# A gated mix of an S5 state-space layer and Hedgehog linear attention: K's weight in halves of rows, four x tiles ahead of V's weight, K products ahead of V's, and a new order list with the later loads in it

## The chip, the core and the metric

The kernel runs on one core of a Trainium2 chip. The metric is the device time of one execution in microseconds (us). The engines are named as the profile names them: PE is TensorE's matmuls and PEld its weight loads, DVE is VectorE, ACT is ScalarE, POOL is GpSimd, SP is SyncE, which here issues DMAs only.

## The reference

Shapes: S = 2048 rows of x, D = 512 columns, state size 512, 32 heads of 16. All inputs and the output are bf16.

```python
x = A_x                                              # [1, 2048, 512]
g = sigmoid((x * gate_w).sum(-1, keepdims=True))
# a: S5. Lam_bar = exp(dt * Lam), B_bar = ((Lam_bar - 1) / Lam)[:, None] * B, all complex
h[t] = Lam_bar * h[t - 1] + x[t] @ B_bar.T
a = 2 * (hseq @ C.T).real + x * Dskip
# b: Hedgehog attention without a mask
q, k, v = split(x @ wqkv)                            # 32 heads of 16
pq, pk = q @ w_phi, k @ w_phi                        # per head
phi_q = [softmax(pq), softmax(-pq)]; phi_k = [softmax(pk), softmax(-pk)]
kv = phi_k.T @ v; z = phi_k.sum(s)
b = ((phi_q @ kv) / (phi_q @ z + 1e-6)) @ wo
out = g * a + (1 - g) * b
```

## The kernel before

**Layout.** x is loaded transposed: 16 DMA transposes of 128 rows each, issued by SyncE, fill xT, [128 partitions, 4 blocks of D, 2048 columns]. The rows are taken by residue: tile ti holds rows 4c + r with r = ti // 4, so that the state-space recurrence is done four steps at a time (the step matrices of Lam_bar's powers are 128x128 diagonals in `dg`, and a scan on DVE carries every fourth step).

**Folded weights.** w_phi is folded into the weights of K and Q before any product: pk = x @ (Wk BD), where BD is block-diagonal with w_phi's 16x16 blocks. For K this is done at the head of the run: `st_B` builds BD out of w_phi (Wc) and a block mask, the steps W0 to W3 (`st_W`) transpose K's natural weight on TensorE into WTk, and f0 to f3 (`st_f`, `fold`) multiply WTk by BD and evict a quarter of Wk2 each. Q's weight is loaded transposed by DMA (WTq) and folded later by w0 to w3.

**Steps and the order list.** Nearly all work is written as generators, one for each step, and the string ORDER says which step is advanced next. A token is a step's name; "@3" gives the PSUM bank it takes, ":D" evicts with DVE instead of ACT, ":A" issues an output store from ACT's queue. Each engine runs its instructions in the order in which the list emits them, without any reordering, except GpSimd, whose order the framework chooses. The steps that matter here:

- V and V2 transpose the small vectors (vec_n: Lambda and log_dt; vec_m: Dskip and gate_w) that GpSimd loads; U, P, P2 to P4 and M compute the state-space parameters from them on DVE, ACT and GpSimd, i0 to i3 the tables of sines and cosines, D the diagonals.
- k0 to k15, v0 to v15, q0 to q15: the products of x tile n with the K, V and Q weights (four matmuls of 512 columns), evicted to Xq, vxb and Xq.
- x, n, e, s with a number: maximum tree, minimum tree, exponentials, sums and normalization of the two softmaxes for a pair of K tiles; A, B and X, N, E, S the same for Q. a0 to a7 accumulate kv, z and the gate's logits in two PSUM banks.
- p (for example p30): LBT = the B matrices (Bn_r, Bn_i) times the diagonals; g: the inputs of the recurrence (xT with BrT, BiT and LBT); z: the scan; h, c, K, r, b: later state-space matrices; y, o, t: the output, 16 tiles.
- F:n issues n spin matmuls of 128 columns on a bank of their own.

**Loads.** All loads are issued ahead of the list. ACT's queue issues K's weight (one DMA of 512 KB into the tile whose name is C2r), w_phi (Wc) and V's weight (Wv). SyncE's queue issues x tiles 0 to 7, the natural B matrices Bn_r and Bn_i (512 KB each), the transposed BrT and BiT (four DMAs each), x tiles 8 to 15, WTq (four; the trace names it H), CrT and CiT (four each) and Wo. SyncE's queue later carries the transposes of the query features (phT), of the attention outputs (oT) and most output stores. GpSimd's queue loads the five small vectors.

Of the kernel before, what the change touches and what calls it, by code (L numbers as in the profile page):

```python
# [26 lines left out]
k3 x0 i1 M v2 V2 v7@1 n0 i2 k2 k7 v3@4 i1 i3 x0 n0 x0 i3 k4 k5 v4@7 i2 n0 i2 k6@2 i2 x1 n0 i3 x1 v0@0 i3 D v4 v3 p22@3  # L27
x1 n1 v5@5 p00@6 x1 n1 x1 i3 x2 L n1 x2 p30@7 v7:D e0 p20@4 x2 D v5 n1 n1 p10@1 p20 n2 p02@5 p30 p10 x2 e0 D n2 s0 v0
v6@4 k6 g101@7 p00 x2 s0 x3 n2 s0 g001@1 g000@0 n2 s0 e1 e1 g001 n2 s1 s0 s0 e2 g100@2 p22 g101 g001 x3 n3 gw s0 e2 n3
k9@6 x3 v6 g100 a0@31 k9 g000 a0 s1 n3 s1 n3 k8@4 g000 x3 s1 s1 s1 g100 k10@6 s2 k8 x3 n3 p12@0 e3 g101 k11@2 s1 e3 x4  # L30
k11 a1 s2 g010@4 n4 k10 a1 s2 g011@7 n4 x4 s2 n4 x4 n4 s3 g010 g011 s2 x4 s3 x4 n4 x5 k12@2 s3 p02 s2 e4 n5 k13@6 x5
e4 s3 x5 s2 n5 s3 g010 g011 s4 a2 k12 g011 x5 n5 s3 p32@5 k13 s4 n5 a2 s3 x5 n5 x6 g010 z0 s4 w0@2 n6 w0 p32 v9@7 w3@6
z0 g111@4 p12 g210@2 n6 w3 s4 e5 e5 w1@5 s5 w1 a3 v8@0 x6 k14@6 s4 z0 g111 g110@5 a3 n6 z0 v9 s5 v8 k15@7 k14 s4 v11@0
z0 x6 x6 z0 k15 s4 n6 w2@6 g110 w2 g201@7 x6 g111 g111 x7 g110 z0 a4 x7 c01@6 z0 g200@4 g110 z1 s5 q1@5 v11 z1 g311@0
s5 x7 s5 n6 s5 c01 n7 g201 e6 z1 g211@6 a4 z1 g201 x7 g200 v10@7 z1 z1 e6 g200 z0 g210 q0@4 g211 g210 s5 q1 n7 v12@5
q0 q3@4 x7 n7 s6 z0 g210 n7 s6 n7 g211 s6 v10 nA xA g301@2 s6 a5 e7 z1 g300@7 g211 q3 e7 nA v14@6 z1 xA z2 nA q2@4 v14
a5 z2 g300 xA s6 s7 q2 z2 s6 s7 z2 g301 g300 xA s7 g311 g301 v12 g310@6 xA g311 z1 nA c11@4 z1 nA eA z2 nB s7 z2 c03@7
c12@2 g310 xB g311 eA q15@5 c12 s6 c03 s7 g310 h01@0 nB q15 g310 sA c10@2 z2 s7 h01 c11 c13@7 xB nB v13@5 z3 xB h11@6
z2 c10 z3 a6 z2 sA z2 h11 q9@0 c02@4 v13 sA q9 xB a6 nB c13 h10@2 q6@5 c02 v15@0 z3 q12@7 q10@6 q8@4 xB v15 sA nB
# [29 lines left out]
def kernel(  # L69
# [45 lines left out]
    def evac(out_ap, in_ap):  # L115
        if sel["eng"] == "act":
            nc.scalar.copy(out=out_ap, in_=in_ap)  # L117
        else:
            nc.vector.tensor_copy(out=out_ap, in_=in_ap)
# [109 lines left out]
    nc.sync.dma_start(out=Bn_r[:], in_=A_B_re.rearrange("(j p) d -> p j d", p=P))  # L229
    nc.sync.dma_start(out=Bn_i[:], in_=A_B_im.rearrange("(j p) d -> p j d", p=P))  # L230
    for kt in range(KT):
        nc.sync.dma_start_transpose(out=BrT[:, kt, :], in_=A_B_re[:, kt * P:(kt + 1) * P])
        nc.sync.dma_start_transpose(out=BiT[:, kt, :], in_=A_B_im[:, kt * P:(kt + 1) * P])
    for ti in range(8, NTI):
        x_load(ti)
    for j in range(KT):
        nc.sync.dma_start_transpose(out=WTq[:, j, :], in_=B_wqkv[:, j * P:(j + 1) * P])
    for kt in range(KT):
        nc.sync.dma_start_transpose(out=CrT[:, kt, :], in_=A_C_re[:, kt * P:(kt + 1) * P])
        nc.sync.dma_start_transpose(out=CiT[:, kt, :], in_=A_C_im[:, kt * P:(kt + 1) * P])  # L240
    nc.sync.dma_start(out=Wo[:], in_=B_wo.rearrange("(k p) n -> p k n", p=P))
# [20 lines left out]
    mask16 = stg.tile([P, 8], F32, name="mask16", bufs=1)  # L262
    nc.vector.tensor_reduce(out=mask16[:], in_=identf[:].rearrange("p (g e) -> p g e", e=16), axis=AX.X, op=ALU.add)
# [12 lines left out]

    def st_W(j):
        pt = bank([P, KT, P], BF16, "ptw")
        for dtile in range(KT):
            nc.tensor.transpose(pt[:, dtile, :], wk_nat[:, dtile, j * P:(j + 1) * P], ident[:])  # L280
        yield
        evac(WTk[:, j, :], pt[:].rearrange("p a b -> p (a b)"))
        yield

    def st_V():
# [460 lines left out]
    def st_t(n):  # L746
# [8 lines left out]
        else:  # L755
# [5 lines left out]
    small1, big1 = (lambda: sk), (lambda: fk)  # L761
    small3, big3 = (lambda: pools["sq"][1]), (lambda: pools["eq"][1])
    st = {"V": st_V(), "V2": st_V2(), "U": st_U(), "P": st_P(), "P2": st_P2(), "P3": st_P3(), "P4": st_P4(), "B": st_B(), "gw": st_gw(),
          "M": st_M(), "D": st_D(), "L": st_L(), "G": st_G(), "Y": st_Y(), "END": st_END()}
    for j in range(4):
        st.update({f"W{j}": st_W(j), f"f{j}": st_f(j), f"w{j}": st_w(j), f"i{j}": st_i(j), f"z{j}": st_z(j), f"r{j}": st_r(j),
                   f"b{j}": st_b(j), f"K{j}": st_K(j), f"p{j}0": st_p(j, 0), f"p{j}2": st_p(j, 2)})
        for e in range(2):
            st.update({f"c{e}{j}": st_c(e, j), f"h{j}{e}": st_h(j, e), f"g{j}0{e}": st_g(j, 0, e), f"g{j}1{e}": st_g(j, 1, e)})
# [57 lines left out]
```

## Time and profile before

| | |
|---|---|
| time, median of 3 runs | 167.55 us (167.46 to 167.75) |
| the profiled execution: span, first to last instruction | 166.1 us |
| median minus span | 1.45 us |
| busy share PE / PEld / DVE / ACT / POOL | 95% / 50% / 87% / 69% / 6% |
| mean granted TensorE clock | 0.994 |
| HBM read / written | 2.64 MB / 2.10 MB |
| K's weight: issue, landing | 0.80 us, 5.15 us |
| V's weight: issue, landing | 1.81 us, 7.70 us |
| x tiles 0, 1, 2, 3: landing | 6.25, 8.58, 10.82, 11.19 us |
| first product of x (v1) on TensorE | 9.67 us |

The span is read from the trace; the device time of a run is a little longer than the span of its instructions. Busy times of matmuls overlap, since they are pipelined: a matmul of 512 columns shows 379 ns, but the next starts 216 ns after it. Engine names with a q (SPq, ACTq) are the queues' instructions, which issue or wait. "xT <- in_A_x_dram" reads: out, in.

### The profile page before, as it was taken

The page shows a single profiled execution, that of the slowest core. Times are in us where ns is not written, and L with a number is a line of the kernel's source. Part 1 is how long each engine was busy: PE and PEld are TensorE (multiplying, and loading weights), DVE is VectorE, ACT ScalarE, POOL GpSimd, SP SyncE. Part 2 cuts the span into 40 slices and gives each one's busy share as a digit, 9 for nine tenths or more (in the row PEclk, how much of TensorE's full clock was granted, in tenths as well). Part 3 has the DMA queues.
Part 4 walks back from the last instruction along what each step waited for, and adds up shares of the span by engine and source line. Part 5 has one row for each costly group of instructions (what it writes and reads, how often), then busy time and mean ns, then how long its engine had stood idle before and what let it go on. Part 6 is the DMA issues. An engine that isn't in the chain of part 4 may idle for free.

```text
span 166.1 us, 3051 instructions
## 1 busy us (share of the span) xinstructions
PE 157.6 (95%) x1088; PEld 82.3 (50%) x1109; DVE 143.7 (87%) x354; ACT 114.8 (69%) x236; POOL 9.6 (6%) x28
## 2 busy tenths in 40 slices
PE   7689999999999999999999999999999999999990
PEld 7444455455465454454454554545446445445440
DVE  4379999999999999999999999999999996818410
ACT  3389999999898268578965966876888356423331
POOL 8218200000000000000000000000000000000000
PEclk9999999999999999999999999999999999999997
DMA  4969945464444200000000019212296585478542
GB/s 111 267 121 281 142 99 97 95 98 95 95 105 85 98 0 6 0 0 0 0 4 0 0 24 181 52 32 63 65 132 154 162 189 129 119 174 216 128 125 95
DMA packets 50830, 15.94 MB, mean 96 GB/s; under 512 B 46208, under 2 KB 50816, under 8 KB 50816
## 3 DMA queue, kind: packets, MB, share of 16 engines
q1 hardware_dynamic: 48064, 13.77, 39.8%
q10 hardware_dynamic: 2592, 1.98, 4.4%
q8 instruction: 8, 0.13, 0.3%
q14 instruction: 6, 0.05, 0.1%
q0 software_dynamic: 160, 0.01, 0.1%
HBM read 2.64 MB, written 2.10 MB: 29 GB/s over the span
## 4 chain that ended last, share of the span: by engine, by line
PE 84%; DVE 8%; DMA 3%; POOL 2%; issue 1%; ACT 1%; POOLq 0%
PE pgq L552 8%; PE py L750 8%; PE pgq L555 8%; PE py L705 8%; PE pq L429 8%; PE py L706 8%; PE pv L429 5%; PE py L712 4%; PE pk L429 4%; DMA vec_n<-in_A_log_dt_dram 3%; PE kvacc L527 3%; PE pn L728 3%; PE pk L674 2%; PE pk L675 2%; DVE psi L406 2%; DVE mxk L464 1%
## 5 line engine op out<-in xcount | busy, mean ns | idle before, releaser
L429 PEld LDWEIGHTS <-xT 128*128 128x128 bf16 x192 | 18.1, 97 | 20.8 <-DMA xT<-in_A_x_dram 0.7
L136 ACT ACTIVATE EEk<-EEk 128x1024 bf16<-128x1024 bf16 x20 | 21.0, 1070 | 0.8 <-DVE EEk L480 0.8
L737 DVE SCALAR_TENSOR_TENSOR on<-pn,RG,rd 128x256 bf16<-128x256 f32 x32 | 14.4, 474 | 3.2 <-ACT rd L136 1.7
L429 PE MATMUL pv<-Wv,xT 128*128 128x512 bf16 x62 | 16.0, 379 | 0.3 <-DMA xT<-in_A_x_dram 0.2
L750 PE MATMUL py<-Wo,oT 128*128 128x512 bf16 x62 | 15.8, 379 | 0.1
L555 PE MATMUL pgq<-xT,LBT 128*128 128x512 bf16 x60 | 15.5, 379 | 0.2
L429 PE MATMUL pq<-Wq,xT 128*128 128x512 bf16 x61 | 15.6, 379 | 0.1
L429 PE MATMUL pk<-Wk,xT 128*128 128x512 bf16 x61 | 15.1, 379 | 0.2
L136 ACT ACTIVATE EEq<-EEq 128x1024 bf16<-128x1024 bf16 x12 | 11.8, 1044 | 3.3 <-DVE EEq L480 3.3
L136 ACT ACTIVATE ld<-pn 128x16 f32<-128x16 f32 x32 | 4.7, 182 | 12.6 <-PE pn L728 12.6
L706 PE MATMUL py<-Wv,H 128*128 128x512 bf16 x31 | 11.7, 379 | 0.1
L705 PE MATMUL py<-Wk,H 128*128 128x512 bf16 x31 | 11.7, 379 | 0.1
L705 PE MATMUL py<-C2r,H 128*128 128x512 bf16 x31 | 11.7, 379 | 0.0
L117 ACT CAST Xq<-pq 128x512 bf16<-128x512 f32 x16 | 9.2, 589 | 3.6 <-PE pq L429 3.4
L117 ACT CAST uv<-pgq 128x512 bf16<-128x512 f32 x16 | 9.3, 588 | 3.4 <-PE pgq L560 2.3
L706 PE MATMUL py<-C2i,H 128*128 128x512 bf16 x30 | 11.4, 379 | 0.1
L756 DVE TENSOR_SCALAR ot<-py,G 128x512 bf16<-128x512 f32 x5 | 3.7, 747 | 8.4 <-PE py L750 8.4
L117 ACT CAST vx<-pv 128x512 bf16<-128x512 f32 x15 | 8.7, 598 | 2.6 <-PE pv L429 2.6
L754 ACT ACTIVATE ot<-py,G 128x512 bf16<-128x512 f32 x11 | 7.4, 678 | 4.5 <-PE py L750 4.5
L117 ACT CAST Xq<-pk 128x512 bf16<-128x512 f32 x16 | 9.2, 601 | 1.4 <-PE pk L429 1.4
L464 DVE TENSOR_TENSOR smk<-smk 128x512 bf16<-128x512 bf16 (+2 forms) x30 | 9.8, 327 | 0.0
L500 DVE TENSOR_TENSOR EEk<-EEk,rck 128x2048 bf16<-128x2048 bf16 x8 | 9.7, 1214 | 0.0
(179 smaller groups left out, 348.6 us busy)
## 6 DMA issues: line engine op xcount, KB each, us to landing
out_dram<-ot SPq DMA_DIRECT2D x9, 128.0 KB, 2.1
out_dram<-ot ACTq DMA_DIRECT2D x7, 128.0 KB, 2.1
C2r<-in_B_wqkv_dram ACTq DMA_DIRECT2D x1, 512.0 KB, 4.4
Wv<-in_B_wqkv_dram ACTq DMA_DIRECT2D x1, 512.0 KB, 5.9
Bn_r<-in_A_B_re_dram SPq DMA_DIRECT2D x1, 512.0 KB, 5.1
Bn_i<-in_A_B_im_dram SPq DMA_DIRECT2D x1, 512.0 KB, 6.0
Wo<-in_B_wo_dram SPq DMA_DIRECT2D x1, 512.0 KB, 3.8
xT<-in_A_x_dram SPq DMA_TRANSPOSE x16, 3.9
```

Source lines behind the costliest of these rows:

```text
L117: nc.scalar.copy(out=out_ap, in_=in_ap)
L136: ins = nc.scalar.activation(**kw)
L429: MM(out=pt[:], lhsT=xT[:, kt, ti * P:(ti + 1) * P], rhs=W[:, kt, :], start=(kt == 0), stop=(kt == KT - 1))
L464: VT(out=t[:], in0=cur[:, :, :, 0:n, :], in1=cur[:, :, :, n:2 * n, :], op=op)
L500: VT(out=E5, in0=E5, in1=rc[:].to_broadcast([P, L, 2 * NB, Dh, 4]), op=ALU.mult)
L552: MM(out=pgq[:], lhsT=BT[:, kt, js], rhs=xT[:, kt, r1 * NC:(r1 + 1) * NC], start=(kt == 0), stop=False)
L555: MM(out=pgq[:], lhsT=LBT_[:, kt, js], rhs=xT[:, kt, (r1 - 1) * NC:r1 * NC], start=False, stop=(r1 == 1 and kt == KT - 1))
L705: MM(out=py[:], lhsT=src[:, j, 0, off:off + P], rhs=cr[:, j, :], start=(j == 0), stop=False)
L706: MM(out=py[:], lhsT=src[:, j, 1, off:off + P], rhs=ci[:, j, :], start=False, stop=False)
L737: nc.vector.scalar_tensor_tensor(out=on[:, 2 * hf:2 * hf + 2].rearrange("p g h e -> p (g h) e"), in0=pns[hf][:, :, 0:Dh], scalar=RG[:, ti: ...
L750: MM(out=py[:], lhsT=oT[:, g, :], rhs=Wo[:, g, :], start=False, stop=(g == HG - 1))
L754: nc.scalar.mul(out=ot[:], in_=py[:], mul=G[:, ti:ti + 1])
```

## The change

- K's weight is loaded in two DMAs of 256 rows each, alone on ACT's queue. Step W(j) now transposes the four blocks of rows 128 j to 128 j + 127 and writes them as a column block of WTk, so W0 and W1 read the first half only, and fold f(d) reads what W(d) wrote alone.
- w_phi goes to SyncE's queue as its first load; x tiles 0 to 3 follow, then V's weight, then x tiles 4 to 7.
- The loads behind these (x tiles 8 to 15, Bn, BrT, BiT, WTq, CrT, CiT, Wo) become steps of the list: l8 to l15, NR and NI, R and I, Q, C, O. They are issued in the list's order: NI l11 NR I3 l10 l15 l9 l8 I1 I0 I2 l13 l12 l14 R3 R1 R0 R2 Q2 Q1 Q0 C5 Q3 C2 C3 C4 C7 C6 C1 C0, and O between the last two phT transposes of the first query tiles.
- The identities are made first on GpSimd, the block mask is bf16, and BD is built by one DVE instruction.
- ORDER is new throughout. At its head, all four folds stand ahead of the transpose V, and TensorE's products begin k0 k1 k2 k3 v1 v0 k5 k4 v7 k7, where they began v1 v2 k1 k0 k5 k3 k2 k7 k4 v7. It has six spins between W0 and W1 and six ahead of v2, in place of eight and one ahead of and behind f3. One V eviction and three output scalings move from DVE to ACT, one fold's eviction from ACT to DVE.

```diff
-B B F:36 W2@0 W2 W1@1 W1:D W0@2 W0:D W3@3 B W3 B F:8 f3@4 F:1 V@5 V f3 f0@6 f2@7 P f0 U P f2 P2 f1@0 U f1 v1@1 P2 v2@2
-k1@3 k0@5 P2 P2 U V2@4 k5@6 k3@7 P P2 P4 P4 U P4 i0 k2@0 P3 P2 P3 k1 i0 k7@3 i1 i0 k0 i0 i0 v1 i2 i1 x0 x0 k4@5 i1 n0
+NI F:36 W0@0 W0 F:6 W1@1 W1 W2@2 W3@3 B f0@4 f0 W2:D f1@5 f2@6 W3:D f3@0 f1 f3 f2:D V@1 k0@2 V P U U P l11 P2 P2 k0 P2
+NR U P2 P2 P4 P3 P k1@3 k1 U P2 P3 V2@4 k2@5 P4 P4 k3@6 k3 i2 v1@0 i1 i2 v0@1 i2 k2 k5@2 i3 i1 k4@3 i1 I3 i2 i2 i3 i3
+x0 l10 k4 v0 v7@6 k7@5 n0 v7 x0 i3 F:6 x1 i3 l15 M k5 i0 n0 i0 n0 v2@3 i0 i0 i0 l9 k7 i1 x0 n1 x0 v2 x1 n0 n1 v4@1 l8
...
-    nc.scalar.dma_start(out=wk_nat[:], in_=B_wqkv[:, D:2 * D].rearrange("(k p) n -> p k n", p=P))
-    nc.scalar.dma_start(out=Wc[:], in_=B_w_phi.rearrange("(k hl) e f -> (hl e) k f", hl=8))
-    nc.scalar.dma_start(out=Wv[:], in_=B_wqkv[:, 2 * D:3 * D].rearrange("(k p) n -> p k n", p=P))
+    for k0 in (0, 2):
+        nc.scalar.dma_start(out=wk_nat[:, k0:k0 + 2, :], in_=B_wqkv[k0 * P:(k0 + 2) * P, D:2 * D].rearrange("(k p) n -> p k n", p=P))
+    nc.sync.dma_start(out=Wc[:], in_=B_w_phi.rearrange("(k hl) e f -> (hl e) k f", hl=8))
...
-    for ti in range(8):
+    for ti in range(4):
         x_load(ti)
-    nc.sync.dma_start(out=Bn_r[:], in_=A_B_re.rearrange("(j p) d -> p j d", p=P))
...
+    nc.sync.dma_start(out=Wv[:], in_=B_wqkv[:, 2 * D:3 * D].rearrange("(k p) n -> p k n", p=P))
+    for ti in range(4, 8):
         x_load(ti)
...
     def st_W(j):
         pt = bank([P, KT, P], BF16, "ptw")
-        for dtile in range(KT):
-            nc.tensor.transpose(pt[:, dtile, :], wk_nat[:, dtile, j * P:(j + 1) * P], ident[:])
-        yield
-        evac(WTk[:, j, :], pt[:].rearrange("p a b -> p (a b)"))
+        for k in range(KT):
+            nc.tensor.transpose(pt[:, k, :], wk_nat[:, j, k * P:(k + 1) * P], ident[:])
+        yield
+        evac(WTk[:, :, j * P:(j + 1) * P], pt[:])
         yield
+
+    def st_l(ti):
+        x_load(ti)
+        yield
...
     def st_B():
-        for kt in range(HG):
-            VT(out=BD[:, kt, :].rearrange("p (g f) -> p g f", f=Dh), in0=Wc[:, kt, :].unsqueeze(1).to_broadcast([P, 8, Dh]),
-               in1=mask16[:].unsqueeze(2).to_broadcast([P, 8, Dh]), op=ALU.mult)
-            yield
+        VT(out=BD[:].rearrange("p k (g f) -> p k g f", f=Dh), in0=Wc[:].unsqueeze(2).to_broadcast([P, HG, 8, Dh]),
+           in1=mask16[:].unsqueeze(1).unsqueeze(3).to_broadcast([P, HG, 8, Dh]), op=ALU.mult)
+        yield
```

More of the change, by code (lines that the diff above doesn't have):

```diff
@@ L30 @@
[L30 to L39, printed above, removed]
@@ new lines @@
+v4 D D x0 k11@6 k11 I1 x2 x1 I0 k6@7 k6 p30@2 p30 p00@5 n1 p00 k10@3 n0 x1 i1 L e0 e0 n2 x2 k10 n2 I2 x3 k15@1 V2 v5@6
+p10@7 gw x2 p10 v1 n1 k9@2 k9 n3 v6@5 x1 k8@4 n2 D x3 p20@3 p20 n1 x2 k8 e1 n3 e1 s0 x2 x3 v5 s0 v3@7 n4 s0 x4 g101@0
+l13 n2 s0 s0 n3 n2 p12@2 n3 x4 g101 v6 s0 g001@3 g001 v3 k15 e2 s1 n4 s1 l12 k13@4 k13 n4 p22@6 k12@5 k12 s0 a0@71 s1
+l14 x3 x5 a0 s1 g011@4 g011 n5 g101 x4 x3 n3 R3 n4 k14@5 n5 x5 n5 s1 x4 e2 s2 s1 s1 s2 R1 x5 n6 p12 s2 g001 n6 s2 R0
+R2 g000@0 e3 e3 g000 g000 s3 n5 x6 n6 s3 s3 a1 a1 Q2 s2 s2 Q1 p32@2 p32 v9@3 v9 g010@0 g010 g010 x4 k14 Q0 p22 s3 g011
@@ L225, in x_load @@
         nc.sync.dma_start_transpose(out=xT[:, :, ti * P:(ti + 1) * P], in_=x_res[ti // 4, ti % 4])
-    for ti in range(8):
-        x_load(ti)
[L229 to L234, printed above, removed]
-        x_load(ti)
[L236 to L241, printed above, removed]
+    make_identity(nc, ident[:])
+    identf = stg.tile([P, P], F32, name="identf", bufs=1)
+    make_identity(nc, identf[:])
+    mask16 = stg.tile([P, 8], BF16, name="mask16", bufs=1)
+    nc.vector.tensor_reduce(out=mask16[:], in_=identf[:].rearrange("p (g e) -> p g e", e=16), axis=AX.X, op=ALU.max)
+    for ti in range(4):
+        x_load(ti)
+    nc.sync.dma_start(out=Wv[:], in_=B_wqkv[:, 2 * D:3 * D].rearrange("(k p) n -> p k n", p=P))
+    for ti in range(4, 8):
+        x_load(ti)
     fk_g = tc.tile_pool(name="featK", bufs=3, reuse_waits="tile")
@@ L261 @@
     nc.vector.memset(eps_p[64:P, :], 0.0)
-    mask16 = stg.tile([P, 8], F32, name="mask16", bufs=1)
-    nc.vector.tensor_reduce(out=mask16[:], in_=identf[:].rearrange("p (g e) -> p g e", e=16), axis=AX.X, op=ALU.add)
     lam, ldt, dsk = vec[:, 0:2, :], vec[:, 2, :], vec[:, 3, :]
@@ L278, in st_W, with st_N, st_BT, st_Q @@
         pt = bank([P, KT, P], BF16, "ptw")
-        for dtile in range(KT):
-            nc.tensor.transpose(pt[:, dtile, :], wk_nat[:, dtile, j * P:(j + 1) * P], ident[:])
+        for k in range(KT):
+            nc.tensor.transpose(pt[:, k, :], wk_nat[:, j, k * P:(k + 1) * P], ident[:])
         yield
-        evac(WTk[:, j, :], pt[:].rearrange("p a b -> p (a b)"))
+        evac(WTk[:, :, j * P:(j + 1) * P], pt[:])
[3 more added lines that the diff above has]
+        yield
+    def st_N(ri):
+        nc.sync.dma_start(out=(Bn_r, Bn_i)[ri][:], in_=(A_B_re, A_B_im)[ri].rearrange("(j p) d -> p j d", p=P))
+        yield
+    def st_BT(kt, ri):
+        nc.sync.dma_start_transpose(out=(BrT, BiT)[ri][:, kt, :], in_=(A_B_re, A_B_im)[ri][:, kt * P:(kt + 1) * P])
+        yield
+    def st_Q(j):
+        nc.sync.dma_start_transpose(out=WTq[:, j, :], in_=B_wqkv[:, j * P:(j + 1) * P])
+        yield
+    def st_C(kt, ri):
+        nc.sync.dma_start_transpose(out=(CrT, CiT)[ri][:, kt, :], in_=(A_C_re, A_C_im)[ri][:, kt * P:(kt + 1) * P])
+        yield
+    def st_O():
+        nc.sync.dma_start(out=Wo[:], in_=B_wo.rearrange("(k p) n -> p k n", p=P))
         yield
@@ L763 @@
     st = {"V": st_V(), "V2": st_V2(), "U": st_U(), "P": st_P(), "P2": st_P2(), "P3": st_P3(), "P4": st_P4(), "B": st_B(), "gw": st_gw(),
-          "M": st_M(), "D": st_D(), "L": st_L(), "G": st_G(), "Y": st_Y(), "END": st_END()}
+          "M": st_M(), "D": st_D(), "L": st_L(), "G": st_G(), "Y": st_Y(), "END": st_END(), "NR": st_N(0), "NI": st_N(1), "O": st_O()}
+    for n in range(8, NTI):
+        st[f"l{n}"] = st_l(n)
     for j in range(4):
-        st.update({f"W{j}": st_W(j), f"f{j}": st_f(j), f"w{j}": st_w(j), f"i{j}": st_i(j), f"z{j}": st_z(j), f"r{j}": st_r(j),
+        st.update({f"W{j}": st_W(j), f"R{j}": st_BT(j, 0), f"I{j}": st_BT(j, 1), f"Q{j}": st_Q(j), f"C{2 * j}": st_C(j, 0), f"C{2 * j + 1}": st_C(j, 1), f"f{j}": st_f(j), f"w{j}": st_w(j), f"i{j}": st_i(j), f"z{j}": st_z(j), f"r{j}": st_r(j),
                    f"b{j}": st_b(j), f"K{j}": st_K(j), f"p{j}0": st_p(j, 0), f"p{j}2": st_p(j, 2)})
```

40 lines of the change are left out of this document (21 added, 19 removed).

## The prediction

> **What bounds the kernel now.** I read the page first, then the busy time by stretches, then the chain that ended last, and then the head of the run engine by engine, with every load's issue and landing.
>
> The page's busy shares and the stretch behind the first V product:
>
> ```profile
> PE 157.6 (95%) x1088; PEld 82.3 (50%) x1109; DVE 143.7 (87%) x354; ACT 114.8 (69%) x236; POOL 9.6 (6%) x28
> ```
>
> ```profile
> 9.67:162.20 152.53, 151.18 (x1013) 76.57 (x1031) 139.95 (x330) 110.70 (x231) 5.25 (x14) 1.00 0.43 90
> ```
>
> In the second view the columns are the stretch, its length, then busy time for TensorE (PE), its weight loads, VectorE (DVE), ScalarE (ACT), GpSimd, the granted clock, the DMA share and GB/s. TensorE is busy 151.18 of 152.53 us at full clock. Matmuls of 512 columns start 0.216 us apart all the way, so the end is simply the start of this dense stretch, plus its work, plus a tail of about 4 us (last matmul at 162.2, span 166.1). DVE is full as well until about 130 us, and ACT is full from 10 to 40 us. They can take back what TensorE wins.
>
> The head of the run on TensorE (start, length, what, idle time before):
>
> ```profile
> 5.20 1.07 PE L280 MATMUL ptw<-ident,C2r 128*128 128x128 bf16 x16 [0.64 <-DMA C2r<-in_B_wqkv_dram]
> ...
> 7.35 0.61 PE L389 MATMUL pf<-BD,Xq 128*128 128x128 bf16 x4 [0.64 <-DVE Xq L119]
> ...
> 8.89 0.16 PE L287 MATMUL pvt<-ident,vec_n 12*128 12x12 bf16 x1 [0.87 <-DMA vec_n<-in_A_log_dt_dram]
> 8.99 0.84 PE L389 MATMUL pf<-BD,Xq 128*128 128x128 bf16 x12
> 9.67 1.03 PE L429 MATMUL pv<-Wv,xT 128*128 128x512 bf16 x3
> 10.87 1.04 PE L429 MATMUL pv<-Wv,xT 128*128 128x512 bf16 x4 [0.17 <-DMA xT<-in_A_x_dram]
> ```
>
> Three of the four folds (12 matmuls) stand behind the transpose of vec_n, which waits for a small GpSimd load; then the second V product waits for x tile 2. The chain of waits says the same, and shows that DVE's own chain starts from the same load:
>
> ```profile
> 3.47 5.29 DMA vec_n<-in_A_log_dt_dram
> ...
> 8.89 0.18 PE pvt L287
> ...
> 9.10 0.18 DVE vec L289
> ...
> 21.39 0.96 DVE dg L381
> ...
> 22.50 0.27 PE pl L539
> ```
>
> **The change, part by part.** The sum is made against the profiled execution, whose span is 166.1 us; the median of the runs, 167.55, is 1.45 us above it, and I keep that offset.
>
> *K's weight in halves.* It landed at 5.15 us (issue 0.80, 4.36 to landing). One 512 KB load alone (Wo) took 3.8, a 128 KB store 2.1, so 256 KB takes about 2.7 alone and the first half lands near 3.5 to 4.0, the second near 5. The 36 spins end at 4.4, so W0 starts about 4.6, W1 after six more spins at 5.2, W2 and W3 at 5.4 to 6.0 (4 transposes 0.22). Evictions of 0.59 (ACT: W0, W1) and 0.33 to 0.37 (DVE: W2, W3) end at 6.5. A fold now needs one W instead of all four. So the folds run from 6.0 to 7.0, and their evictions (three on ACT at 0.5, one on DVE at 0.69) give the whole folded K weight at about 7.9; before, the last started at 10.38 and ended at 10.98. The block mask becomes one DVE instruction instead of four (0.2 each) and runs while DVE is idle; its bound is 0.3 to 0.6 us, from the 128x512 rows of both DVE rates (0.34, 0.67), and it ends near 4.5, before the first fold needs it.
>
> *The folds leave the gap behind vec_n.* K's first product is queued behind the vec_n transpose. GpSimd has the same instructions ahead of its third load (two memsets, two selects, iota, two loads), so I leave that landing at 8.76. The first K product then starts at 8.97 instead of the first V product at 9.67: **-0.70**. The halves themselves are thus hidden behind vec_n; what counts is that all folds are done by then.
>
> *Four x tiles, then V's weight.* Tile 2 landed at 10.82, 7.2 us after its issue, while tile 6 took 2.9: V's weight was in the way. Behind K's weight alone, tiles 0 to 3 (issues 1.4, 2.7, 4.1, 5.5) land within 5 us of issue, by 6.4, 7.7, 9.1 and 10.5, against needs at 8.97, 9.83, 10.8 and 11.7. The wait (second product due at 10.53, ran at 10.87) goes: **-0.34**. V's weight, issued at 6.8, lands at 10.6 to 12.0 (3.8 as Wo, 5.1 as Bn_r); its first product is due at 12.5. What is late next is tile 7, below.
>
> *Six spins before v2* are new work inside the dense stretch: 6 x 0.056 = **+0.33**. The sum of shorter steps is otherwise the same: counted out of both lists, the matmuls behind the first product are equal in number and shape.
>
> *The loads as list steps.* SyncE issues the same loads without a wait, 1.31 us for each transposed one, but w_phi and V's weight now pass through it (0.53 + 0.58). Each later load is pushed by 1.2, or by 1.9 if the first tile behind V's weight takes 1.91 to issue as BrT did behind two such loads. The needs, from summing the new list's matmuls from 8.97: tile 11 at 19.8, Bn at 21.5, tile 10 at 22.3, all BiT at 29.3, all BrT at 38.6, Q's weight at 45.7. The landings, with the latencies of the same place before, are 18.5 to 19.9, 20.0 to 21.5, 21.0 to 22.9, 27.4 to 29.2, 37.1 to 38.3, 44.3 to 45. All touch their need at the upper end, so I count **0** and keep +0.6 for the range. Wo moves behind a wait (the phT transposes, near 98 us); it is needed at 117, and one more transpose is queued behind it: 0.
>
> *The new order elsewhere.* I summed DVE's rows along the new list from 9.10: the softmax of pair 0 ends 1.1 us before kvacc needs it, the first three diagonals 1.0 before p30, the later pairs 1.1 to 4.5, the scans 2.8 to 4.2, the query features 5 to 8. ACT, summed the same way, evicts k13 at 35.9 where its bank is due at 36.0: the thinnest cover; if ACT runs late there, TensorE pays all of it. A bank's next use comes at least 1.6 us after its last matmul (0.87 before). DVE loses three output scalings (0.73 each) to ACT in the last stage, where both are idle for half the time: 0. The tail (last product, one ACT scaling 0.69, one store) is unchanged.
>
> Sum: -0.70 - 0.34 + 0.33 = -0.71; span 165.4, **166.8 us**.
>
> A row and a rule on vec_n. Summed by half microseconds, the trace's packets show ACT's queue moving 289 KB between 5.5 and 6.5 us (V's weight), SyncE's none, and GpSimd's 160 packets coming only from 6.4 to 8.0; its five loads all took 5.2 to 6.0 to land. That looks as if V's weight held the others back. The Trainium skill, page "DMA: Bandwidth & Descriptors", section "Queues, rings and completion order", says that each DMA engine takes turns between the queues that have work, a packet at a time; by that rule V's weight holds nobody back and vec_n stays at 8.76, which is my sum. By the row it comes earlier, which is the first rival.
>
> **The rivals.**
>
> *vec_n lands early.* With V's weight out of the way its packets could come with the first half of K's. Bound: the folded K weight at 7.9, so the first K product starts no earlier than about 8.0: -0.97 more, 165.9 us. Against it: the five latencies hardly differ, though the first was issued when the queues were empty, and the needs of the loads move forward too, so tile 7 (due at 15.0 then) takes much of it back.
>
> *Late tile 7, the slower side.* Tile 7 was issued at 10.21 and landed at 15.31, just ahead of Bn_r, and the first load behind the two Bn took even longer (the loads by their issue, with the us to landing, from two short windows; then SyncE's queue):
>
> ```profile
> xT<-in_A_x_dram SPq DMA_TRANSPOSE x1, 5.1
> ...
> BrT<-in_A_B_re_dram SPq DMA_TRANSPOSE x1, 6.8
> ```
>
> ```profile
> 11.52 0.58 SPq L229 DMA_DIRECT2D Bn_r<-in_A_B_re_dram  x1
> ...
> 12.69 1.91 SPq L232 DMA_TRANSPOSE BrT<-in_A_B_re_dram  x1
> ```
>
> Pushed by 1.86 with the same 5.1 it lands at 17.2, where v7 is due at 15.98: a stall of 1.2, and 167.55 - 0.71 + 1.2 = 168.0. It decides from a landing behind 17.0. Against it: only one Bn follows it directly now, and tile 6 took 2.9, with which it lands at 15.0. Every other load that touches its need would cost in the same way.
>
> *Given back.* Smaller waits of 0.4 to 1.0 in all (tile 7 at 16.5, the Bn weights, ACT around 36): 167.2 to 167.8.
>
> *The clock falls back.* TensorE now idles from about 7.0 to 8.9 us with nothing between. The spins of the timeline start 0.107 us apart until 3.75 and 0.056 after 3.84: a cold half-rate phase of some 2.7 us here. If the idle time brought such a phase back, 2.7 us of products at half rate lose 1.35: 168.2. Against it: idle times of 0.64, 0.64 and 0.87 between 4.6 and 8.9 did not. The Trainium skill, page "TensorE: Matmul & The Clock Gate", section "HAM oscillation — how this bites in real kernels", puts the danger at idle gaps of more than about 3.4 us, which speaks against this rival.
>
> **How the numbers follow.** A measurement of this kernel can tell about 0.2% (0.34 us) from no change. Chances: the forecast (dense from 9, 0.4 to 1.1 won) 0.42; vec_n early 0.14; given back to within 0.34 us 0.13; late tile 7 or another late load 0.28; the clock 0.03. Faster 0.56, same 0.13, slower 0.31. The range runs from 165.8 (vec_n early) to 168.3 (late tile 7 and a few tenths of a second wait); the forecast's own is 166.4 to 167.2.
>
> **What would show it.** Right: the first K product at 8.9 to 9.0 directly behind vec_n, the folds over by 7.2, no wait at the second and third product, TensorE gapless from there. An early vec_n shows as a first product near 8. Late loads show as idle time ended by an xT or Bn load before v7, k11, p30 or k10; a slow ACT as idle time ended by an eviction near 36 us; the clock as products 0.43 apart behind 9 us. The prediction is wrong if TensorE's idle time behind the first K product sums to more than 1 us.

## The result: 166.74 us, where 166.8 was predicted, by other terms than the sum's

The changed kernel takes 166.74 us (median of 4 runs, 166.55 to 167.07); the kernel before, run beside it, 167.65. The ratio is 0.9939, with a 95% interval of 0.9917 to 0.9960. The profiled execution took 166.79 us with a span of 165.1 (before 166.1). On a second chip, further below, the same kernel came to 0.9901 (0.9866 to 0.9935). Five of the twelve runs of e3, further below, show a mean granted clock of 0.986 to 0.989 and take 0.7 to 2.2 us more than the others on average; among the runs above 0.99 its ratio is 1.008 instead of 1.0106.

The time is the predicted one. Its working is not: the prediction named its own test, that it is wrong if TensorE's idle time behind the first K product sums to more than 1 us, and that sum is 1.31 us by the idle times shown below, 2.06 by the delays that they stand for.

The changed kernel's busy shares, then the stretch from its first product on (columns as in the view before):

```profile
PE 157.7 (96%) x1093; PEld 82.6 (50%) x1112; DVE 141.9 (86%) x348; ACT 116.7 (71%) x239; POOL 9.1 (5%) x28
```

```profile
7.07:161.20 154.13, 151.77 (x1019) 76.95 (x1037) 138.79 (x329) 112.76 (x234) 4.71 (x14) 1.00 0.45 94
```

TensorE's work behind the first product is what it was (151.77 us busy, 151.18 before), but the stretch starts 2.60 us earlier and is 1.6 us longer. TensorE's rows show where (start, length, what, idle time before it and what ended it):

```profile
1.11 3.61 PE L805 MATMUL spin<-fillw 128*128 128x128 bf16 x36 [1.11 <-DVE fillw L155]
4.56 0.39 PE L269 MATMUL ptw<-ident,C2r 128*128 128x128 bf16 x4
...
5.12 0.83 PE L269 MATMUL ptw<-ident,C2r 128*128 128x128 bf16 x12
5.79 1.24 PE L401 MATMUL pf<-BD,Xq 128*128 128x128 bf16 x16
6.96 0.18 PE L300 MATMUL pvt<-ident,vec_n 12*128 12x12 bf16 x1
7.07 2.00 PE L441 MATMUL pk<-Wk,xT 128*128 128x512 bf16 x7
...
13.06 1.90 PE L441 MATMUL pk<-Wk,xT 128*128 128x512 bf16 x8 [0.34 <-DMA xT<-in_A_x_dram]
15.24 1.04 PE L441 MATMUL pv<-Wv,xT 128*128 128x512 bf16 x4 [0.27 <-DMA xT<-in_A_x_dram]
...
38.88 0.60 PE L564 MATMUL pgq<-xT,BrT 128*128 128x512 bf16 x2 [0.38 <-DMA BrT<-in_A_B_re_dram]
...
127.89 1.04 PE L762 MATMUL py<-Wo,oT 128*128 128x512 bf16 x4 [0.32 <-DMA oT<-on]
```

The transposes of K's weight and the folds are over before vec_n's transpose, as planned, but that transpose runs at 6.96 and no longer at 8.89, since vec_n lands at 6.61 us. Then four waits follow: for x tile 5 (13.06), x tile 7 (15.24), the last BrT (38.88) and, in the output, an oT transpose (127.89). A start's delay against the regular 0.216 us spacing is a little more than the idle time in brackets: 0.50, 0.44, 0.54 and 0.48; with 0.10 around vec_m's transpose (the second vector's, between two products) that makes the 2.06.

The chain that ended last, its shares and three of its pieces, says the same from the other end:

```profile
PE 71%; SPq 20%; DMA 5%; issue 1%; ACT 1%
```

```profile
9.74 2.27 SPq L225
...
33.01 1.26 SPq L283
34.32 4.51 DMA BrT<-in_A_B_re_dram
```

Up to 38.8 us it is now SyncE, issuing loads without a pause (the shares of the chain before name no SyncE queue at all); x tile 6's issue alone took 2.27 us, behind V's weight. SyncE's rows of that stretch:

```profile
1.31 5.21 SPq L225 DMA_TRANSPOSE xT<-in_A_x_dram  x4
6.57 0.58 SPq L234 DMA_DIRECT2D Wv<-in_B_wqkv_dram  x1
7.19 6.13 SPq L225 DMA_TRANSPOSE xT<-in_A_x_dram  x4
13.37 0.58 SPq L279 DMA_DIRECT2D Bn_i<-in_A_B_im_dram  x1
```

### The profile page after: what moved, and what is told of

The parts are those of the page before. It is cut to its first block, busy times and chain, and to the rows that moved or that the text cites. A ratio compares the mean times of both kernels' runs of the same rounds, so it can differ in the third digit from the quotient of the medians.

```text
span 165.1 us, 3046 instructions
## 1 busy us (share of the span) xinstructions
PE 157.7 (96%) x1093; PEld 82.6 (50%) x1112; DVE 141.9 (86%) x348; ACT 116.7 (71%) x239; POOL 9.1 (5%) x28
## 4 chain that ended last, share of the span: by engine, by line
PE 71%; SPq 20%; DMA 5%; issue 1%; ACT 1%
SPq L225 13%; PE pq L441 8%; PE py L762 8%; PE py L718 8%; PE py L717 7%; PE pgq L567 7%; PE pgq L564 7%; SPq L283 5%; PE py L724 4%; PE pv L441 4%; DMA BrT<-in_A_B_re_dram 3%; PE kvacc L539 2%; PE pn L740 2%; PE pk L686 2%; PE pk L687 2%; DMA oT<-on 2%
## 5 line engine op out<-in xcount | busy, mean ns | idle before, releaser
L749 DVE SCALAR_TENSOR_TENSOR on<-pn,RG,rd 128x256 bf16<-128x256 f32 x32 | 13.9, 477 | 7.7 <-ACT rd L136 7.5
L136 ACT ACTIVATE EEk<-EEk 128x1024 bf16<-128x1024 bf16 x20 | 20.5, 1082 | 0.0
L567 PE MATMUL pgq<-xT,LBT 128*128 128x512 bf16 x63 | 16.2, 379 | 0.1
L441 PE MATMUL pk<-Wk,xT 128*128 128x512 bf16 x62 | 15.6, 379 | 0.4 <-DMA xT<-in_A_x_dram 0.3
L441 PE MATMUL pv<-Wv,xT 128*128 128x512 bf16 x61 | 15.3, 379 | 0.3 <-DMA xT<-in_A_x_dram 0.3
L766 ACT ACTIVATE ot<-py,G 128x512 bf16<-128x512 f32 x14 | 9.5, 683 | 8.3 <-PE py L762 8.3
L718 PE MATMUL py<-Wv,H 128*128 128x512 bf16 x32 | 12.1, 379 | 0.2
L718 PE MATMUL py<-C2i,H 128*128 128x512 bf16 x31 | 11.7, 379 | 0.1
L117 ACT CAST vx<-pv 128x512 bf16<-128x512 f32 x16 | 9.5, 602 | 2.8 <-PE pv L441 2.4
L717 PE MATMUL py<-C2r,H 128*128 128x512 bf16 x30 | 11.4, 379 | 0.1
L717 PE MATMUL py<-Wk,H 128*128 128x512 bf16 x29 | 11.0, 379 | 0.0
L762 PEld LDWEIGHTS <-oT 128*128 128x128 bf16 x64 | 6.0, 98 | 7.1 <-DMA oT<-on 0.7
```

The costliest lines, as they stand in the source:

```text
L136: ins = nc.scalar.activation(**kw)
L441: MM(out=pt[:], lhsT=xT[:, kt, ti * P:(ti + 1) * P], rhs=W[:, kt, :], start=(kt == 0), stop=(kt == KT - 1))
L567: MM(out=pgq[:], lhsT=LBT_[:, kt, js], rhs=xT[:, kt, (r1 - 1) * NC:r1 * NC], start=False, stop=(r1 == 1 and kt == KT - 1))
L717: MM(out=py[:], lhsT=src[:, j, 0, off:off + P], rhs=cr[:, j, :], start=(j == 0), stop=False)
L718: MM(out=py[:], lhsT=src[:, j, 1, off:off + P], rhs=ci[:, j, :], start=False, stop=False)
L749: nc.vector.scalar_tensor_tensor(out=on[:, 2 * hf:2 * hf + 2].rearrange("p g h e -> p (g h) e"), in0=pns[hf][:, :, 0:Dh], scalar=RG[:, ti: ...
```

## The experiments

All ratios are against the kernel before, run on the same chip. The changed kernel itself ran on two of the chips only, so e1 to e6 and e11 to e15 are set against it by ratios from different chips and by single profiled executions. For every profiled execution except those of e8 and its sister, which run at half rate for a while, the same sum holds: the start of the last matmul is the first product's start, plus TensorE's waits behind it (counted as above), plus the work, which is 151.2 to 151.3 us with the old list, 151.5 to 151.7 with the new one and 151.3 with the new one without the six spins (e2). In the table "full rate" is when TensorE's granted clock rises, from each trace.

| kernel | ratio (95%) | full rate | first product | waits | last matmul |
|---|---|---|---|---|---|
| before | 1 | 3.8 | 9.67 | 0.86 | 161.78 |
| changed | 0.9939 (0.9917 to 0.9960) | 4.1 | 7.07 | 2.06 | 160.80 |
| changed, second chip | 0.9901 (0.9866 to 0.9935) | 5.4 | 7.70 | 0.77 | 160.09 |
| e1: V's weight behind K's on ACT's queue | 0.9945 (0.9921 to 0.9970) | 6.6 | 9.13 | 0.39 | 161.07 |
| e2: no spins ahead of v2 | 0.9987 (0.9952 to 1.0022) | 5.5 | 8.02 | 3.14 | 162.43 |
| e3: new head of loads, old list | 1.0106 (1.0066 to 1.0145) | 6.0 | 11.21 | 0.88 | 163.33 |
| e4: w_phi behind K's on ACT's queue | 0.9908 (0.9876 to 0.9940) | 6.7 | 8.60 | 0.93 | 161.12 |
| e6: K's weight in one DMA | 0.9910 (0.9883 to 0.9937) | 6.1 | 8.02 | 0.98 | 160.65 |
| e8: V's weight by ACT, as a step | 1.0598 (1.0551 to 1.0645) | lost | 17.30 | see text | 170.88 |
| e10: t4 behind y9 | 0.9892 (0.9864 to 0.9920) | 3.9 | 7.05 | 1.91 | 160.56 |
| e11: e4 and e10 | 0.9906 (0.9883 to 0.9929) | 6.6 | 8.30 | 0.32 | 160.21 |
| e14: V's weight by GpSimd, and e10 | 0.9889 (0.9865 to 0.9912) | 6.3 | 8.07 | 0.10 | 159.88 |
| e15: e14 with 12 spins fewer | 0.9898 (0.9872 to 0.9925) | 5.4 | 7.04 | 2.14 | 160.84 |

**V's weight back behind K's (e1).** Does V's weight hold back the small loads?

```diff
+    nc.scalar.dma_start(out=Wv[:], ...)      # behind K's two halves
-    nc.sync.dma_start(out=Wv[:], ...)        # between x tiles 3 and 4
```

> V's weight goes back to ACT's queue, directly behind K's halves; all else is the changed kernel. Theory (V's weight behind K's holds the other queues): GpSimd's packets come only when V's weight is through, vec_n lands at 8.2 to 8.8 instead of 6.61 and the first K product starts at 8.5 to 9.0 instead of 7.07; SyncE's later loads go 0.6 earlier (last BrT at 38.2), but TensorE then reaches them at about 39.2, so 0.2 to 0.5 slower than the changed kernel, 166.9 to 167.3. Rival (the queues take turns, what brought vec_n forward is the order of the GpSimd instructions or the first loads on SyncE): vec_n stays near 6.6, first product near 7.1, and the 0.6 on SyncE is won: 166.1 to 166.3.

The queues' packets between 5 and 6 us, first of the changed kernel, then of e1 (q1 is SyncE's queue, q0 GpSimd's, q10 ACT's; packets, MB, share of 16 engines):

```profile
q1 hardware_dynamic: 473, 0.11, 53.2%
q0 software_dynamic: 77, 0.00, 7.4%
```

```profile
q10 hardware_dynamic: 168, 0.17, 81.5%
q1 hardware_dynamic: 44, 0.01, 4.7%
```

While V's weight moves, GpSimd's queue moves nothing and SyncE's a tenth of the other kernel's packets. vec_n lands at 8.90 instead of 6.61, x tile 0 at 7.99 instead of 5.41, and the transposes wait as they did before:

```profile
9.03 0.16 PE L300 MATMUL pvt<-ident,vec_n 12*128 12x12 bf16 x1 [0.87 <-DMA vec_n<-in_A_log_dt_dram]
9.13 1.90 PE L441 MATMUL pk<-Wk,xT 128*128 128x512 bf16 x8
```

So the first product is 2.06 us later, yet the last matmul only 0.27, and the ratio is near that of the changed kernel's first comparison: SyncE is 0.58 us shorter, the last BrT lands at 35.98 instead of 38.83, and the waits are 0.39 instead of 2.06. By these two executions the early first product was worth almost nothing by itself. The theory is met in vec_n and the first product to about 0.1 us, not in the last BrT, which it had at 38.2.

SyncE's shorter list does not explain that landing alone. Of the 2.85 us, 1.10 is the earlier issue (33.22 instead of 34.32) and 1.75 the time from issue to landing (2.76 instead of 4.51). In the changed kernel a packet of 16 KB on the DMA queue that the profile names instruction starts at 35.39, while that load is under way; in e1 one starts at 36.88, when it has landed. In the ten traces with the new list (e8 and its sister apart), the last BrT takes 3.9 to 4.9 us in the six where such a packet starts 1.1 to 2.4 us after its issue, and 2.7 to 2.9 in the four (e1, e4, e11, e14) where it starts later or finds the load nearly landed. That is a coincidence of times; no run moved the packet alone.

**No spins ahead of v2 (e2).**

```diff
-x0 l10 k4 v0 v7@6 k7@5 n0 v7 x0 i3 F:6 x1 i3 ...
+x0 l10 k4 v0 v7@6 k7@5 n0 v7 x0 i3 x1 i3 ...
```

> The six spins ahead of v2 are left out; nothing else changes. Theory (SyncE's issue order up to the last BrT sets the end): TensorE reaches the BrT wait 0.33 earlier and waits 0.33 longer, last BrT at 38.8 as before, time the same within 0.1: 166.7. Rival (TensorE's work from the first product sets the end): 0.33 faster, 166.4.

Missed by both: 0.9987, above e1 and e4 on the same chip, and no run of it is under 167.2 us. On DVE the spins are absorbed as expected (step N1 starts at 101.03, in the changed kernel at 100.97), but 1.0 us of waits for Bn_r and x tiles stands ahead of 24 us, and two waits of 2.0 us in all at 128 us, for a phT and an oT transpose that took 5.7 us each to land; e15 shows a wait of that kind again, below.

**The new head of loads with the old list (e3).** Kernel before, with K's halves, w_phi and V's weight on SyncE as in the change, and nothing else of it.

```diff
+    for k0 in (0, 2):
+        nc.scalar.dma_start(out=wk_nat[:, k0:k0 + 2, :], ...)
+    nc.sync.dma_start(out=Wc[:], ...)
...
+    nc.sync.dma_start(out=Wv[:], ...)        # behind x tile 3
```

> The kernel before with its own list, and only the head of the loads changed: K's weight in halves on ACT's queue, w_phi, four x tiles, V's weight, four x tiles on SyncE's. Theory: vec_n lands near 6.6 and the folds are over by 8, but the list's first product is V's, whose weight lands at 10.5, so the first product starts at 10.5 instead of 9.67, the wait for tile 2 (0.33) goes, and SyncE's later loads come 1.2 later: 0.4 to 1.0 slower than the kernel before, 168.0 to 168.7. Rival (the loads bring the gain, the list adds little): first product near 8, 1.0 faster than before, 166.6.

Slower by 0.8% to 1.1%, in the direction expected and more. V's products still lead, V's weight lands at 11.16, and the first product moves from 9.67 to 11.21; the last matmul moves by the same 1.55. Here, where the waits are as before (0.88 and 0.86), the first product counts one to one. Alone, the new loads lose; with the new list, whose K products stand ahead of V's, they gain.

**w_phi on ACT's queue (e4).**

```diff
-    nc.sync.dma_start(out=Wc[:], ...)
+    nc.scalar.dma_start(out=Wc[:], ...)      # behind K's halves
```

> w_phi is issued from ACT's queue behind K's halves instead of first on SyncE's. Theory (SyncE's queue sets the end): every SyncE load goes 0.5 earlier, last BrT at 38.3 instead of 38.8; BD is built 1 to 2 later and the first K product starts at 7.4 to 8.2 instead of 7.07, which the waits for tiles 5 and 7 take up: 0.3 to 0.5 faster than the changed kernel, 166.3. Rival (the first product sets the end): 0.4 to 1.0 slower, 167.1 to 167.7.

w_phi lands at 6.72 instead of 3.90, so the block matrix and the folds are late (first product 8.60), but SyncE's list is 0.5 us shorter: last BrT at 36.04, no wait for a load, only 0.22 for a quarter of the folded weight within the first product and 0.61 at 128 us. The time is no worse than the changed kernel's.

**The changed kernel on the chip of the next three.**

> The changed kernel once more, beside the three that follow, so that all four share one chip. Both theories expect 166.6 to 166.9 us, 0.992 to 0.996 of the kernel before, with TensorE's waits at x tiles 5 and 7 (0.4 to 0.5 each), at the last BrT tile (0.3 to 0.6) and at the output product of tile 4 of the output order, near 128 us (0.3 to 0.6).

The ratio is lower than expected, 0.9901, and the waits differ: 0.25 at tile 5, 0.28 for Bn_r, 0.14 at tile 10, none at tile 7, BrT or oT. The first product is at 7.70, since TensorE's full rate came at 5.4 us and not at 4.1 (its 36 spins took 4.02 us instead of 3.61). One kernel's executions thus spread over 0.6 us at the head, and here the waits take up the difference and more.

**t4 behind y9 (e10).**

```diff
-... S2 S2 t4 o7 o7 X3 X3 S2 t3 o7 o7 y9@2 N3 o5 t5 ...
+... S2 S2 o7 o7 X3 X3 S2 t3 o7 o7 y9@2 t4 N3 o5 t5 ...
```

> The changed kernel with one token moved: the output product t4 (which waits for oT near 127.9 us) stands behind the first four matmuls of y9 (0.86 us), which wait for nothing. Late-landing theory: t4 then starts near 128.3, after oT's landing at 127.8 to 128.2, the wait of 0.5 is gone and the last matmul and the end come 0.3 to 0.5 earlier, 166.2 to 166.5, with nothing changed ahead of 127 us. Rival (the wait there is slack that some later wait takes up, such as the next query features): the wait shows up again behind 129 us and the time stays at 166.7.

The rows show the mechanism: y9's matmuls (L717, L718) run ahead of t4, which starts at 128.51 without a wait, and none follows:

```profile
127.40 0.42 PE L740 MATMUL pn<-KVm,phT 128*128 128x68 bf16 x8
127.65 0.38 PE L717 MATMUL py<-Wk,H 128*128 128x512 bf16 x1
...
128.51 1.89 PE L762 MATMUL py<-Wo,oT 128*128 128x512 bf16 x7
```

Its time, though, is the changed kernel's on that chip (0.9892 and 0.9901): that kernel's profiled execution had no oT wait either. The wait is there in some executions only. The early waits go with an early first product: at 7.05, as in the changed kernel's first trace (7.07), they are back, 0.50 at tile 5, 0.44 at tile 7, 0.29 at tile 11 and 0.58 at the last BrT.

**V's weight issued by ACT behind W1 (e8), and with t4 behind y9.**

```diff
-NI F:36 W0@0 W0 F:6 W1@1 W1 W2@2 ...
+NI F:36 W0@0 W0 F:6 W1@1 W1 VW W2@2 ...
+    def st_VW():
+        nc.scalar.dma_start(out=Wv[:], ...)
+        yield
```

> V's weight is issued by ScalarE behind W1's eviction (near 5.7 us) instead of by SyncE between x tiles 3 and 4; nothing else differs from the changed kernel. Late-landing theory (the lead of the early first product is lost in waits for loads that SyncE issues late, and near 128 us in the wait for an oT transpose that DVE and SyncE set): every SyncE issue behind x tile 3 comes 0.6 to 1.5 us earlier, the waits at tiles 5 and 7 and at BrT fall from 1.5 to under 0.5 us together, the first product stays at 7.0 to 7.6; but the oT wait near 128 us grows from 0.5 to 1.0 to 1.5, since oT does not come earlier, so the time stays within 0.3 us of the changed kernel. Rival (the start of the first product and the sum of the early waits set the end): 1 us less waiting early is 1 us less at the end, 165.6 to 165.9.

> Both edits: V's weight issued by ScalarE behind W1's eviction, and t4 behind the first four matmuls of y9. Late-landing theory: the early waits fall by 1.0 to 1.5 us and the oT wait is covered by 0.86 us of other matmuls, so the two edits give more than their sum: 165.4 to 166.1. If DVE, which is full from 7 to 123 us, sets other steps too, less: 166.0 to 166.4, with waits for DVE's results between 40 and 127 us. Rival (the early waits alone count): the same as with V's weight moved alone, less nothing.

Both are slower by 6%: 1.0598 and 1.0582 (1.0542 to 1.0623). The built program gives the DMAs of both hardware queues eight semaphores in turn, and the new issue got the one that Bn_i's load carries. So ACT waited for Bn_i's landing at 16.20 with three folds' evictions queued behind that issue. ACT's waits, then TensorE:

```profile
ACT Wk L117 <- DMA Bn_i<-in_A_B_im_dram: 9.4, 1, 9.4
```

```profile
17.30 2.35 PE L444 MATMUL pk<-Wk,xT 128*128 128x512 bf16 x5 [8.97 <-ACT Wk L117]
```

As a test of the placement they say nothing. They do show the fourth rival's mechanism, which no other run does: after 8.97 us of idle time the products run at half rate, until 20.4 in e8 (the seventh column of values is the granted clock) and 22.8 in its sister:

```profile
17.30:20.40 3.10, 2.88 (x7) 0.94 (x7) 1.73 (x13) 1.71 (x5) 0.29 (x2) 0.50 1.32 200
20.40:25.00 4.60, 4.48 (x22) 1.81 (x21) 4.60 (x12) 4.20 (x9) 2.46 (x3) 1.00 1.44 175
```

The Trainium skill, page "TensorE: Matmul & The Clock Gate", section "HAM oscillation — how this bites in real kernels", puts the danger at idle gaps over about 3.4 us; 0.87 us did nothing in the kernel before and 8.97 did it here, so these runs agree and say nothing of the lengths between. The granted clock itself fell 1.8 us after TensorE's last matmul in e8, sooner than the page's figure, and 4.7 us after it in the sister.

**V's weight issued by GpSimd, with t4 behind y9 (e14).**

```diff
-    nc.sync.dma_start(out=Wv[:], ...)        # between x tiles 3 and 4
+    nc.gpsimd.dma_start(out=Wv[:], ...)      # behind vec_n and vec_m
```

> V's weight is issued by GpSimd behind its five small loads (near 5 us, when GpSimd has nothing to do until 9 us) instead of by SyncE between x tiles 3 and 4, and t4 stands behind the first four matmuls of y9. Late-landing theory: the first product stays at 7.0 to 7.7, since vec_n's packets go ahead; SyncE issues everything behind x tile 3 by 0.6 us or more earlier; the waits at x tiles 5 and 7 and at BrT fall from 1.5 us to under 0.5 in sum, and near 128 us at most 0.5 is left; the last matmul near 159.5 to 160.1, 0.984 to 0.989 of the kernel before, 0.4 to 0.9 us under the changed kernel. Rival (DVE, full from 7 to 123 us, takes back what TensorE wins): the early waits vanish as well, but new waits for DVE's results stand between 40 and 129 us, and the ratio stays at 0.990 to 0.994.

The theory's run: SyncE issues the eight x tiles in one row, V's weight lands at 9.73, the last BrT at 35.94, and no wait of any kind is left behind the first product but the 0.10. Part of that may be the later first product itself, 1.0 us behind the changed kernel's; e15 shows how much.

```profile
1.30 10.89 SPq L225 DMA_TRANSPOSE xT<-in_A_x_dram  x8
```

The last matmul is at 159.88, within the theory's 159.5 to 160.1. The ratio, 0.9889, is at the theory's edge, because the first product is at 8.07: vec_n landed at 6.93 but TensorE was late with spins and transposes at half rate:

```profile
1.11 4.02 PE L805 MATMUL spin<-fillw 128*128 128x128 bf16 x36 [1.11 <-DVE fillw L155]
4.92 0.63 PE L269 MATMUL ptw<-ident,C2r 128*128 128x128 bf16 x4
...
7.96 0.18 PE L300 MATMUL pvt<-ident,vec_n 12*128 12x12 bf16 x1
8.07 2.00 PE L441 MATMUL pk<-Wk,xT 128*128 128x512 bf16 x7
```

**K's weight in one DMA (e6).**

```diff
-    for k0 in (0, 2):
-        nc.scalar.dma_start(out=wk_nat[:, k0:k0 + 2, :], ...)
+    nc.scalar.dma_start(out=wk_nat[:], ...)
```

> K's weight comes in one DMA instead of two halves; the steps, the list and all else are the changed kernel's. It lands near 4.9 to 5.1 us instead of 4.06 and 4.73, so the first transposes start 0.4 to 0.6 later, and the folds are over at 7.3 to 7.5 instead of 6.96. My reading (with vec_n landing at 6.6 to 7.5 the folds do set the first product, so the halves count at the head): first product at 7.4 to 7.9; but the late loads take that back at x tiles 5 and 7, so the end moves by 0.0 to +0.3 us. Rival, as in the prediction (the halves are hidden behind vec_n): first product unchanged. Rival that the head counts one to one: +0.4 to +0.6 us.

Inconclusive at the head: the whole weight lands at 4.81, but the full rate came at 6.1 and the last of the 36 spins starts at 4.82, so W0 starts at 4.93, as in e14 with the halves (4.92). When the rate comes late the halves are hidden behind the spins. In time it is 0.9910 against 0.9889 and 0.9906 on the same chip: no difference that can be told.

**w_phi on ACT's queue with t4 behind y9 (e11).**

```diff
-    nc.sync.dma_start(out=Wc[:], ...)
+    nc.scalar.dma_start(out=Wc[:], ...)      # behind K's halves
-... S2 S2 t4 o7 o7 X3 X3 S2 t3 o7 o7 y9@2 N3 ...
+... S2 S2 o7 o7 X3 X3 S2 t3 o7 o7 y9@2 t4 N3 ...
```

> w_phi on ScalarE's queue behind K's halves (as in the run before with that edit alone, whose one wait left was 0.61 us for oT near 128 us), and t4 behind the first four matmuls of y9. Late-landing theory: no wait at x tiles, BrT or oT is left, so the last matmul comes 0.4 to 0.6 us earlier than with w_phi moved alone: 0.985 to 0.989 of the kernel before. Rival (the oT wait is slack that later waits take up): the same ratio as with w_phi moved alone, 0.991, with a new wait behind 129 us.

In the profile nearly as the theory has it: no wait for a load or an oT, only the 0.10 and 0.22 for a quarter of the folded weight as in e4; last matmul 0.91 us earlier than in e4. The ratio, 0.9906, is e4's; the gain is not shown in the time.

**Fewer spins at the head (e15).**

```diff
-NI F:36 W0@0 W0 F:6 W1@1 W1 W2@2 ...
+NI F:30 W0@0 W0 W1@1 W1 W2@2 ...
```

> The run with V's weight on GpSimd's queue and t4 behind y9, with 30 spins ahead of W0 instead of 36 and none between W0 and W1. In the runs so far TensorE's full rate came between 3.8 and 6.8 us; where it came late, the 36 spins ended at 4.82 instead of 4.4, W1 had six more at half rate ahead of it, and the first product came at 7.7 to 8.3 instead of 7.05 (vec_n had landed at 6.6 to 7.5). Theory (late full rate, not vec_n, sets the first product in those executions): W0 starts at 4.1 to 4.3 and the last transpose ends by 6.0 even at half rate, the first product comes at 7.0 to 7.3, tied to vec_n at 6.6 to 7.0; with V's weight off SyncE's queue the loads follow (at most 0.3 of waits at x tiles and BrT), at most 0.4 at oT near 127 us; last matmul 158.9 to 159.7, 0.983 to 0.988 of the kernel before. Rival (DVE and the oT transposes set the stage near 127 us whenever TensorE comes there earlier than 127.5): the head wins up to 0.9 us and the wait for oT or phT there takes it back, last matmul 159.7 to 160.1, ratio 0.988 to 0.991. Rival (fewer spins make the full rate come later, or lose it): products 0.43 us apart behind the first one, slower than with 36.

The theory's head came true: at a full rate from 5.4 us on, the first product is at 7.04 instead of 7.7 to 8.3. Its waits for loads did not: 0.41 at tile 3, which now lands behind V's weight at 10.29, 0.22 at tile 7 and 0.10 at tile 10, where at most 0.3 was expected. They are still half of the changed kernel's 1.47 up to the last BrT at the same first product, and none is for BrT. Then the first rival came true: the lead is lost at 127 us, and 0.9898 is within its range, though the last matmul, at 160.84, is later than its 160.1. TensorE's row there, and the DMA view from 121 to 128 us of e15 (busy share in 40 slices, in tenths; then one queue):

```profile
127.67 0.43 PE L740 MATMUL pn<-KVm,phT 128*128 128x68 bf16 x8 [1.15 <-DMA phT<-EEq]
```

```profile
DMA  3029950007999900000001000899999900994997
...
q8 instruction: 1, 0.02, 1.7%
```

The DMA engines nearly stand still from about 123.5 to 125.4 us, with a phT (issued 121.47, landing 127.62) and an oT transpose under way. At 122.73 the queue named instruction starts a packet of 16 KB, which takes 1.9 us. In every trace but those of e8 and its sister, which run 10 us late, such a packet falls between 122.3 and 125.9 us, and transposes in flight around it take 3.3 to 6.2 us to land instead of 2.3 to 2.9. That the one causes the other is argued from this and from the last BrT in e1; no run moved or removed it by itself, so what makes e2 slower stays open that far.

## Why the prediction was right in the time and wrong in the sum

By the profiled executions: first product 2.60 us earlier, waits 1.20 us longer (0.86 to 2.06), work 0.42 longer, so the last matmul comes 0.98 earlier (161.78 to 160.80) and the span is 1.0 shorter. The sum on record was -0.70, -0.34 and +0.33.

- **K's halves, the folds, the block mask.** Right: 4.06 and 4.73 for the landings, W0 at 4.56, W1 at 5.12, folds 5.79 to 6.9, folded weight done at 7.8 (all as worked out, to 0.3 us). The block mask took 0.69, a little over its bound of 0.6. "Hidden behind vec_n" fell with the next point: vec_n's transpose now stands directly behind the folds, without a wait.
- **"I leave that landing at 8.76": the step that failed.** vec_n landed at 6.61. The trace's row had said so (GpSimd's packets only behind V's weight), and the sum took the rule instead. The Trainium skill, page "DMA: Bandwidth & Descriptors", section "Queues, rings and completion order", has the engines take turns between queues; e1 shows that here 168 packets of one queue went with 44 of the second and none of the third. That none of the third went for a whole microsecond, with its loads issued, is not taking turns. The measurement decides: the head's term was -2.60 instead of -0.70. Even the rival's bound of 8.0 was too cautious, since a product needs each fold's quarter only as it comes to it.
- **Four x tiles ahead of V's weight.** Right for tile 2, which landed at 7.86; the -0.34 is in the waits. "What is late next is tile 7" was right too, with tile 5 beside it: 0.94 together, where the slower rival had 1.2.
- **"So I count 0" for the later loads: failed.** Two things were wrong. The needs came earlier than assumed: tiles 5 and 7, landing at 13.02 and 15.19, would have been in time with a first product at 8.97 (v7 was due at 15.98 then). And BrT landed at 38.83 against an estimate of 37.1 to 38.3, while its need, 38.6 in the estimate, was 38.3; with the 2.7 to 2.9 us to landing of e1, e4, e11 and e14 instead of 4.51 it would have been in time. These four have a shorter SyncE list and no wait for BrT; the list and the 16 KB packet both differ in them. In e15, which has the shorter list and the packet (4.30 us to landing), the last BrT lands at 37.79 and no wait follows; no run has the longer list without the packet.
- **The output stage.** The 0.48 at oT was not foreseen at all.
- **The spins, ACT's cover at 36 us, the tail.** Spins +0.33 of the 0.42 (e2 has that much less work); no wait for ACT; last matmul to end of span 4.3 us as before.
- **The clock.** No fallback in the changed kernel. What was not foreseen is that its full rate starts anywhere from 3.8 to 6.8 us over these traces, and that the new head's spins, transposes and folds, with vec_n no longer behind them, carry this to the first product.

Three rivals were thus partly true at once: vec_n early, tile 7 late, and smaller waits giving it back. The number was met because the two failed terms, 1.9 us too little at the head and some 1.5 us too little in waits, nearly cancel; the remaining 0.3 us of span is made up by the offset from span to time, 1.7 us here where 1.45 was kept. That an early start comes back as waits was a rival on record; that it came back to within 0.1 us of the forecast is luck. e1 shows the cancelling between two executions. On its cause, e14 and e15 agree: with V's weight off SyncE's queue the waits for loads are gone at a first product of 8.07, and halved at one of 7.04.

Of the versions run, e14 has the lowest ratio, 0.9889 (0.9865 to 0.9912). It beats the kernel before, and its interval lies under that of the changed kernel's first comparison (0.9917 to 0.9960, another chip); from the changed kernel's second (0.9901), and from e10 (0.9892), which moves t4 alone, it can't be told. So what V's weight on GpSimd's queue is worth in time is not shown.

## What to carry to other kernels

When the first work starts earlier, every load's need moves with it: redo each slack with the new start, and look for the queue whose issues have no pause, since its last landings, and not the head alone, can then set the time. Where a row of the trace and a general rule speak against each other about the same queues, take the row. And a DMA issued from a compute engine's instruction stream can carry a wait for an unrelated load, with everything behind it on that engine.

## What the runs showed of the hardware that was not expected

- A 512 KB load on ACT's queue kept SyncE's transposed tiles and GpSimd's 1 KB loads almost still: x tile 0 landed at 7.99 instead of 5.41 us, vec_n at 8.90 instead of 6.61. w_phi, 16 KB, landed at 6.72 us behind K's weight and at 3.90 on SyncE's queue.
- TensorE's full rate came between 3.8 and 6.8 us after the start, with the same 36 spins from 1.11 us on.
- Most transposes of phT and oT land in 2.3 to 2.9 us, but in 3.3 to 6.2 where a 16 KB instruction packet falls among them; the last BrT, likewise, in 2.7 to 2.9 or 3.9 to 4.9. That the packet is the cause is argued, not shown.
- After TensorE fell idle, the granted clock fell 1.8 us later in one run and 4.7 in another, and stayed at half for 10.24 us in both.
